# A convolution and SwiGLU kernel: one unit's x loads twelve steps later, their second copy twenty steps later, and the start's filler matmuls regrouped from six and a short one, then three, to eight, then four

## The chip, the cores and the metric

The kernel runs on one core of a Trainium2 chip. The metric is device microseconds (us) of one execution; the number given for a kernel is the median of its runs. TensorE is called PE in the profile, VectorE DVE, ScalarE ACT, GpSimd POOL and SyncE SP. POOL and SP both issue transfers; SP's transfers are issued in the order of its program, and so are POOL's, between POOL's arithmetic.

## The reference

A causal convolution with seven taps, whose taps are a softmax per head, runs over the sequence; its result goes through a gated feed-forward block.

```python
w = weight - np.max(weight, axis=-1, keepdims=True)      # weight: 8 heads x 7 taps
w = np.exp(w)
w = w / (np.sum(w, axis=-1, keepdims=True) + 1e-09)
x_pad = np.concatenate([np.zeros((B, pad, D)), x], axis=1)   # x: 8 x 4096 x 192, pad 6
x_unf = x_pad[:, idx, :].reshape(B, S, K, H, group)
out = np.einsum('hk,bskhg->bshg', w, x_unf)
...
g = x @ w_gate                                            # 192 -> 1536
silu = g * (1.0 / (1.0 + np.exp(-g)))
val = x @ w_val
return (silu * val @ w_out)                               # 1536 -> 192
```

## The kernel before, in words

The 32,768 tokens are cut into 16 units of 2,048 tokens, and each unit into four blocks of 512. For each block the feed-forward part takes twelve steps, one for each 128 of the 1,536 inner features, so that there are 768 steps in all; they are counted by n, and a unit is 48 steps. Block 0 starts at n = 0, unit 1 at n = 48, block 5 at n = 60, unit 2 at n = 96.

A step (`gate_val`, line 765) is six matmuls (line 774: gate and val, three slices of 64 channels each), a Silu on ACT (line 783, kept as `silu[n]`) and a product on DVE (line 785). Every third step a `slot` (line 833) adds a group of down-projection matmuls (line 800); the fourth slot of a block evicts the result (lines 858 and 859) and SP writes it out (line 862). PE takes everything in program order.

The convolved x of each unit is made in one of three ways.

- Unit 0 is made at the start by PE (`early`, `eturn`), with taps spread into a matrix (`spread_taps`, line 287, and `make_wide`, line 315).
- Unit 2 alone is convolved by PE with a banded matrix (`conv_half`, line 450): POOL loads overlapping windows of x into the tile x16 (`load_x`, line 129, transfers of line 98: one of 26 x 192 elements after a small memset, one of 32 x 39 x 192, one of 32 x 40 x 192), SP copies each of its two 32-row parts to the next 32 rows (`dup_x`, line 144, two transfers of 480 KB, line 148), and at n = 58 and n = 70 PE multiplies (line 466), which ACT and DVE evict into tm (line 483). POOL then copies 64 columns of tm (`conv_dup`, line 494), SP writes tm to HBM (`conv_out`, lines 502 and 510) and reads it back transposed (`fetch`, line 524) as the xc that the steps from n = 96 on read.
- Unit 1 and units 3 to 15 are "pooled": POOL's queue casts x into HBM (`cast_x`, line 580), SP reads it back transposed (line 595) and joins halves (line 599), and ACT, DVE and POOL multiply and add the taps (`conv_job`, line 614; POOL's additions are line 627, its products line 642). A unit has six such jobs. For unit 1 POOL takes four taps of the six that are added in each job. SP then moves the results into place (`place`, line 687, four transfers per block, line 701). The first of them for block 4 and block 5 reach SP's program at n = 38 and n = 48.

The order on each engine is written out by hand: the helper `seq` (line 73) ties each instruction to the one recorded before it on the same engine. The step loop (line 896) decides where something stands: it calls `gate_val`, the slot, `pooled_work` (line 740) and then the loads of x16, the copies `dup_x` and the jobs of `plan`. An instruction of a late engine therefore runs later than its n suggests: POOL and SP lag behind PE. The loads carry a wait for `silu[n - 1]`, so that they don't start early.

At the start PE runs filler matmuls on a zero tile (`keep_warm`, line 872) while the taps are computed: six of 512 columns and one of 128 ahead of `spread_taps`, three of 256 columns behind it, ahead of `make_wide`.

Of the kernel before, what the change touches and what calls it, by code (L numbers as in the profile page):

```python
# [10 lines left out]
def kernel(  # L11
# [23 lines left out]
    P = 128  # L35
# [37 lines left out]
    def seq(i):  # L73

        e = i.ins.engine
        if e in last_on:
            tc.add_manual_dep(i.ins, last_on[e].name, NOSYNC, reason="order")
        last_on[e] = i.ins
        return i
# [64 lines left out]
    def dup_x(u, queue=None):  # L144
        for r in range(2):
            p0 = Q * r
            seq(
                (queue or nc.sync).dma_start(
                    out=x16[u][p0 + 32 : p0 + 64], in_=x16[u][p0 : p0 + 32]
                )  # L150
            )
# [135 lines left out]
    def spread_taps():  # L287
        bank = apool.tile([P, TB], fp32, tag="acc0", name="tapbank")
        for a in range(2):
            seq(  # L290
                nc.tensor.matmul(
                    bank[:, a * H : a * H + H],
                    split[:, a].rearrange("h k q -> h (k q)"),
                    eye[0:H, 0:H],
                    start=(a == 0),
                    stop=True,
                    skip_group_check=True,
                )
            )
        seq(nc.vector.tensor_copy(tap, bank[:, 0 : 2 * H]))  # L300
        seq(
            nc.vector.tensor_tensor(
                spread.rearrange("p j a h -> p j (a h)"),
                eyes,
                tap.unsqueeze(1).to_broadcast([P, 16, 2 * H]),
                op=ALU.mult,
            )
        )
# [6 lines left out]
    def make_wide():  # L315
        banks = [
            ppool.tile([P, TB], fp32, tag=tag, name="taps") for tag in ("gate", "val")
        ]
        for n in range(4):
            c0 = 16 * 2 * H * (n % 2)  # L320
            seq(
                nc.tensor.matmul(
                    banks[n // 2][:, c0 : c0 + 16 * 2 * H],
                    shift[:, n].rearrange("p r i -> p (r i)"),
                    spread.rearrange("p j a h -> p (j a h)"),
                    start=(n % 2 == 0),
                    stop=True,
                    skip_group_check=True,
                )
            )  # L330
        seq(nc.vector.tensor_copy(pf, pid))
        for h0 in (0, 4):
            for n in range(2):
                seq(
                    (nc.scalar.copy, nc.vector.tensor_copy)[n](
                        wide[:, :, h0 : h0 + 4, 32 * n : 32 * n + 32],
                        banks[n].rearrange("p (j a h) -> p a h j", a=2, h=H)[
                            :, :, h0 : h0 + 4, :
                        ],
                    )  # L340
                )
        seq(
            nc.vector.tensor_scalar(
                ident, cid, scalar1=pf, scalar2=None, op0=ALU.is_equal
            )
        )
# [80 lines left out]
    def eturn(b, where):  # L427
        xc[b] = []
        for k in range(SL):
            t = cpool.tile([P, XW], fp16, tag=f"xc{k}", name=f"xc{k}", bufs=6)  # L430
            pool, tag = where[k]
            bank = pool.tile([P, EG, P], fp16, tag=tag, name="turn")
            for g in range(EG):
                seq(
                    nc.tensor.transpose(  # L435
                        bank[:, g, :], tme[b][:, g, Q * k : Q * k + P], ident
                    )
                )
            seq(
                (dve, act, dve)[k](  # L440
                    t.rearrange("p (g c j) -> p g c j", c=2, j=EO),
                    bank.rearrange("p g (c q) -> p g c q", c=2)[:, :, :, 0:EO],
                )
            )
            xc[b].append(t)
# [94 lines left out]
    def make_picks():  # L540
        for name in which:
            pick[name] = small(f"pick_{name}", [H, P], fp16)
            seq(
                nc.vector.scalar_tensor_tensor(
                    pick[name], which[name], float(grp), above[name],
                    op0=ALU.is_lt, op1=ALU.mult,
                )
            )
# [154 lines left out]
    def pooled(u):  # L703
        return u in POOLED
# [60 lines left out]
    def gate_val(n):  # L765
        b, j = divmod(n, NCH)
        g = ppool.tile([P, TB], fp32, tag="gate", name="gate")
        v = ppool.tile([P, TB], fp32, tag="val", name="val")
        m, e = divmod(j, E)
        for k in range(SL):  # L770
            for half, o in ((0, g), (1, v)):
                p0 = Q * half
                seq(
                    nc.tensor.matmul(  # L774
                        o,
                        w16[m][p0 : p0 + Q, (k + half) % SL, e::E],
                        xc[b][k][p0 : p0 + Q, 0:TB],
                        start=(k == 0),
                        stop=(k == SL - 1),
                    )  # L780
                )
        sg = hpool.tile([P, TB], fp16, tag="sig", name="sig", bufs=3)
        silu[n] = seq(nc.scalar.activation(sg, g, AF.Silu)).ins  # L783
        hj = hpool.tile([P, TB], fp16, tag="h", name="h", bufs=15)
        seq(nc.vector.tensor_tensor(hj, sg, v, op=ALU.mult))  # L785
        hbuf[n] = hj
# [85 lines left out]
    def keep_warm(count, width=TB):  # L872
        for _ in range(count):
            seq(
                nc.tensor.matmul(  # L875
                    warm[:, 0:width], fill,
                    fill.unsqueeze(1).to_broadcast([P, width // P, P]),
                    start=True, stop=True, skip_group_check=True,
                )
            )  # L880

    gate_bank, val_bank = (ppool, "gate"), (ppool, "val")
    acc_banks = (apool, "acc0"), (apool, "acc1")
    keep_warm(6)
    keep_warm(1, P)
    spread_taps()
    keep_warm(3, 2 * P)
    make_wide()
    early(0, (gate_bank, gate_bank, val_bank))
    eturn(0, (*acc_banks, gate_bank))  # L890
# [5 lines left out]
    for n in range(n_steps):  # L896
        b, j = divmod(n, NCH)
        u, ls = divmod(n, ustep)
        work = None
        if n in (12, 19):  # L900

            def work(e=2 if n == 12 else 3):
                early(e, (gate_bank, gate_bank, val_bank))

        at = (10, 22)
        if u + 1 < NU and not pooled(u + 1) and ls in at:

            def work(u=u, hh=at.index(ls)):
                conv_half(u + 1, hh)

        gate_val(n)
        if n == 6:
            early(1, (*acc_banks, gate_bank))
        elif n == 8:
            eturn(1, (*acc_banks, gate_bank))
        elif n in (9, 12, 15, 17):
            k = {9: 1, 12: 2, 15: 3, 17: 4}[n]
            slot(k, 0, silu[n - 1 if k == 4 else n - 2], work)
        elif j % 3 == 1 and n > 18:
            if j == 4 and act_steps and act_steps[0][0] < (  # L920
                dve_steps[0][0] if dve_steps else n_jobs[0]
            ) + 3:
                act_steps.pop(0)[1]()
            k = {1: 3, 4: 4, 7: 1, 10: 2}[j]
            slot(k, b - 1 if j < 7 else b, silu[n - 2], work)
        if n == 18:
            eturn(2, (*acc_banks, gate_bank))
        elif n == 20:
            eout(3)
        elif n == 21:  # L930
            efetch(3)
        if n == 10:
            make_picks()
        if n == 13:
            make_channel_taps()
        pooled_work(n, j, work is not None)
        if u + 1 < NU and not pooled(u + 1):
            if ls == at[0]:
                conv_dup(u + 1)
            if ls == at[1]:  # L940
                for m in range(2):
                    conv_out(u + 1, m)
            if ls == at[1] + 1:
                for m in range(2, 8):
                    conv_out(u + 1, m)
            if ls in range(28, 40, 3):
                fetch(UB * (u + 1) + (ls - 28) // 3)
        if u + 2 < NU and not pooled(u + 2):
            if ls == (16 if u == 0 else 1):
                x16_tile(u + 2)  # L950
                load_x(u + 2, 0, silu[n - 1])
            if ls == (18 if u == 0 else 5):
                load_x(u + 2, 1, silu[n - 1])
            if ls == (31 if u == 0 else 26):
                dup_x(u + 2)
        for job in plan.pop(n, ()):
            job()
    b = n_blocks - 1
# [41 lines left out]
```

## Time and profile before

| what | value |
|---|---|
| median of 5 runs | 780.39 us (779.04 to 782.48) |
| the profiled execution's own time | 780.39 us |
| its span | 778.6 us |
| granted TensorE clock over the span | 0.999 |
| PE / DVE / ACT / POOL busy | 99% / 88% / 78% / 84% |
| POOL busy in 36 to 56, 56 to 76, 76 to 96 us | 19.32, 19.33, 19.33 of 20.00 us |
| PE busy in 112 to 120 us | 5.62 of 8.00 us |
| the chain that ended last | PE 93%, POOL 3%, SP's queue 1%, DMA 1% |

The span begins at the program's first instruction and ends with its last one; the remaining 1.8 us of the execution's time lie around it. A busy share of PE counts matmuls that are pipelined, so that 99% does not mean that nothing can be gained in a stage; waits and the order of time show where a stage is held up. Rows of a timeline give the start, the length, the engine ("SPq" for SP's queue of instructions, where the length is that of the issue and not of the transfer), the line, the operation, the tiles and how many instructions were merged; a bracket gives the idle time before the row and what ended it.

### The profile page before, as it was taken

Reading aid. Unit: us, or ns where it says so; the run is one execution under the profiler, and the core shown is the slowest. Engines: PE = TensorE matmul, PEld = TensorE weight load, DVE = VectorE, ACT = ScalarE, POOL = GpSimd, SP = SyncE. Lnnn points to the kernel's source line nnn. Section 1 sums busy time; section 2 is a strip of 40 time slices with the busy share of each in tenths; the row PEclk is TensorE's granted clock in tenths of the full one; section 3 lists DMA queues with packets and bytes.
Section 4 is the critical chain, followed back from the end, with each engine's and each line's share of the span. In section 5 each row is a group of like instructions: output and inputs, shape, how many; then the busy total and the mean of one; then the engine's idle time right before and its main releaser. Section 6 shows DMA issues by size and latency. Waiting matters only on the chain.

```text
span 778.6 us, 27795 instructions
## 1 busy us (share of the span) xinstructions
PE 767.4 (99%) x11113; PEld 590.5 (76%) x11113; DVE 687.5 (88%) x1036; ACT 609.9 (78%) x1075; POOL 651.1 (84%) x600
## 2 busy tenths in 40 slices
PE   8999989999999999999999999999999999999997
PEld 5667657777777777777777777777777777777776
DVE  7687879999999999999999999999999999997775
ACT  6676868888888788788788788788888888886664
POOL 8299987989999999899999999999999989994000
PEclk9999999999999999999999999999999999999999
DMA  9975384752544546354442653634353452221211
GB/s 159 143 126 134 80 145 104 155 116 76 122 101 99 107 87 117 78 122 93 104 112 58 136 104 84 122 85 105 91 118 91 108 111 60 70 68 37 70 56 43
DMA packets 135678, 77.78 MB, mean 100 GB/s; under 512 B 82036, under 2 KB 135036, under 8 KB 135036
## 3 DMA queue, kind: packets, MB, share of 16 engines
q1 hardware_dynamic: 127884, 61.22, 34.9%
q0 software_dynamic: 7664, 14.79, 11.6%
q8 instruction: 87, 1.43, 0.8%
q14 instruction: 43, 0.35, 0.1%
HBM read 29.58 MB, written 37.58 MB: 86 GB/s over the span
## 4 chain that ended last, share of the span: by engine, by line
PE 93%; POOL 3%; SPq 1%; DMA 1%; issue 0%; ACT 0%; DVE 0%; POOLq 0%
PE gate L774 50%; PE acc L800 31%; PE val L774 11%; POOL total L627 2%; SPq L524 1%; POOL piece L642 1%; PE warm L875 0%; DMA xc<-scr 0%; PE turn L435 0%; PE cv L377 0%; SPq L701 0%; PE acc L821 0%; DMA pxc<-pxc 0%; POOL y L627 0%; DVE h L785 0%
## 5 line engine op out<-in xcount | busy, mean ns | idle before, releaser
L785 DVE TENSOR_TENSOR h<-sig,val 128x512 f16<-128x512 f16 x768 | 496.7, 684 | 82.8 <-PE val L774 49.8
L783 ACT ACTIVATE sig<-gate 128x512 f16<-128x512 f32 x768 | 446.9, 600 | 152.3 <-PE val L774 125.4
L774 PE MATMUL gate<-pxc,w 64*128 64x512 f16 x2016 | 471.8, 376 | 0.8 <-DMA pxc<-pxc 0.8
L774 PE MATMUL val<-pxc,w 64*128 64x512 f16 x2016 | 471.6, 376 | 0.3 <-DMA pxc<-pxc 0.3
L774 PEld LDWEIGHTS <-w 64*128 64x128 f16 x4608 | 319.9, 110 | 131.3 <-issue 4.3
L800 PEld LDWEIGHTS <-h 64*128 64x128 f16 x6096 | 273.7, 94 | 44.6 <-ACT sig L783 11.8
L800 PE MATMUL acc<-wo,h 64*128 64x192 f16 x6096 | 303.3, 243 | 1.5 <-ACT sig L783 1.2
L627 POOL TENSOR_TENSOR total<-total,part 128x512 f32<-128x512 f32 x136 | 173.1, 1273 | 31.9 <-DVE total L652 23.5
L627 POOL TENSOR_TENSOR total<-total,piece 128x512 f32<-128x512 f32 x122 | 170.8, 1400 | 10.2
L642 POOL TENSOR_SCALAR piece<-x,both_taps 128x512 f32<-128x512 f16 x206 | 168.9, 820 | 0.0
L652 DVE SCALAR_TENSOR_TENSOR total<-x,both_taps,total 128x512 f32<-128x512 f16 x162 | 168.4, 1040 | 0.0
L677 ACT ACTIVATE part<-x,both_taps 128x512 f32<-128x512 f16 x136 | 97.6, 718 | 0.0
L627 POOL TENSOR_TENSOR pxc<-total,piece 128x512 f16<-128x512 f32 x56 | 72.3, 1292 | 4.7
L774 PE MATMUL gate<-xc,w 64*128 64x512 f16 x288 | 68.9, 377 | 2.4 <-DMA xc<-scr 2.4
L774 PE MATMUL val<-xc,w 64*128 64x512 f16 x288 | 68.7, 377 | 0.1
L677 ACT ACTIVATE total<-x,both_taps 128x512 f32<-128x512 f16 x84 | 60.5, 720 | 4.6 <-DMA x<-xs 3.3
L627 POOL TENSOR_TENSOR y<-total,piece 128x512 f16<-128x512 f32 x28 | 46.6, 1663 | 2.3
L859 DVE COPY o_sb<-acc 128x384 f32<-128x384 f32 x63 | 34.7, 551 | 0.0
L858 ACT COPY o_sb<-acc 128x384 f32<-128x384 f32 x63 | 29.6, 470 | 0.1
L98 POOL DMA_DIRECT2D x<-in_x_dram x3 | 2.3, 777 | 9.2 <-ACT sig L783 9.2
L580 POOL DMA_DIRECT2D xs<-in_x_dram x14 | 7.8, 557 | 0.0
L98 POOL DMA_DIRECT2D xe<-in_x_dram x9 | 6.1, 685 | 0.1
(68 smaller groups left out, 61.3 us busy)
## 6 DMA issues: line engine op xcount, KB each, us to landing
out_dram<-o_sb SPq DMA_DIRECT2D x63, 384.0 KB
pxc<-pxc SPq DMA_DIRECT2D x112, 64.0 KB
pxc<-y SPq DMA_DIRECT2D x112, 64.0 KB
xs<-in_x_dram POOLq DMA_DIRECT2D x8, 774.0 KB, 7.1
xs<-in_x_dram POOLq DMA_DIRECT2D x6, 768.0 KB, 6.9
x<-x SPq DMA_DIRECT2D x28, 66.0 KB
x<-xs SPq DMA_TRANSPOSE x112
x<-x SPq DMA_DIRECT2D x2, 480.0 KB
```

The source lines that it names most:

```text
L98: nc.gpsimd.dma_start(out=t[p0 + i0 : p0 + i1, w0 - at : w1 - at, :], in_=bass.AP(tensor=x_flat.tensor, offset=(t0 + size * w0 - pad + i0) ...
L580: nc.gpsimd.dma_start(out=flat[skip * D : rows * D].rearrange("(a n) -> a n", n=n), in_=bass.AP(tensor=x_flat.tensor, offset=(u * UT - XP ...
L627: nc.gpsimd.tensor_tensor(job["dst"] if k == K - 1 else total, total, part, op=ALU.add)
L642: nc.gpsimd.tensor_scalar(part, shifted(k), scalar1=job["tap"][:, k : k + 1], scalar2=1.0, op0=ALU.mult, op1=ALU.mult,)
L652: nc.vector.scalar_tensor_tensor(job["total"], shifted(k), job["tap"][:, k : k + 1], job["total"], op0=ALU.mult, op1=ALU.add,)
L677: nc.scalar.activation(part, shifted(k), AF.Copy, scale=job["tap"][:, k : k + 1])
L774: nc.tensor.matmul(o, w16[m][p0 : p0 + Q, (k + half) % SL, e::E], xc[b][k][p0 : p0 + Q, 0:TB], start=(k == 0), stop=(k == SL - 1),)
L783: silu[n] = seq(nc.scalar.activation(sg, g, AF.Silu)).ins
L785: seq(nc.vector.tensor_tensor(hj, sg, v, op=ALU.mult))
L800: nc.tensor.matmul(acc[b][bank][:, s, :], hj[p0 : p0 + Q, ts(2 * bank + s, P)], wo16[p0 : p0 + Q, j, :], start=(not second and j == 0 and ...
L858: seq(nc.scalar.copy(o_sb[:, 0:2, :], acc[b][0]))
L859: seq(nc.vector.tensor_copy(o_sb[:, 2:4, :], acc[b][1]))
```

## The change

The two loads of unit 2's x move from n = 16 and n = 18 to n = 28 and n = 30; the second copy of it moves from n = 31 to n = 51, seven steps ahead of the first matmuls that read it. At the start PE's fillers become eight of 512 columns ahead of the taps, and four of 256 columns behind them. No arithmetic of the result is changed.

```diff
-    keep_warm(6)
-    keep_warm(1, P)
+    keep_warm(8)
     spread_taps()
-    keep_warm(3, 2 * P)
+    keep_warm(4, 2 * P)
     make_wide()
...
         if u + 2 < NU and not pooled(u + 2):
-            if ls == (16 if u == 0 else 1):
+            if ls == (28 if u == 0 else 1):
                 x16_tile(u + 2)
                 load_x(u + 2, 0, silu[n - 1])
-            if ls == (18 if u == 0 else 5):
+            if ls == (30 if u == 0 else 5):
                 load_x(u + 2, 1, silu[n - 1])
-            if ls == (31 if u == 0 else 26):
+            if u and ls == 26:
                 dup_x(u + 2)
+        if n == 51 and not pooled(2):
+            dup_x(2)
         for job in plan.pop(n, ()):
             job()
```

In the order of the built program, POOL's memset and three loads stood behind the cast of unit 1 and ahead of the first addition of unit 1's first job; they now stand behind the last addition of its second job (the one that writes y for blocks 4 and 5) and ahead of the first addition of its third (block 5). SP's two copies stood ahead of the four transfers that place block 4; they now stand behind those of blocks 4 and 5 and behind one transposing read of unit 3.

## The prediction

> **What bounds the kernel now.** I read the page first, then the chain of work that ended last, then the timelines of POOL, SP's queue and PE over the first 120 us, where everything that the change touches lies. The page says that PE is the bound over the whole span, so the end moves only if some wait of PE moves.
>
> ```profile
> PE 767.4 (99%) x11113; PEld 590.5 (76%) x11113; DVE 687.5 (88%) x1036; ACT 609.9 (78%) x1075; POOL 651.1 (84%) x600
> ```
>
> The chain between 75 and 120 us (start, length, what) shows the last such wait.
>
> ```profile
> 104.80 5.92 SPq L524
> 110.76 2.80 SPq L524
> 113.60 2.69 DMA xc<-scr
> 116.33 0.37 PE gate L774
> ```
>
> After 116.33 the chain is PE alone up to the end. PE waits there, at n = 96, for unit 2's xc, read by the transposes of line 524. Whatever changes the time of that matmul changes the end by as much; earlier waits count only if they reach it. Without a wait its gate matmul would have come at about 113.4 (the gates before it, at 112.33, 112.55 and 112.76, lie 0.215 apart, and it is the third one on), so PE has 2.9 us of slack there.
>
> What sets the data's time is POOL. Its timeline (start, length, line, tiles, idle time before):
>
> ```profile
> 17.46 0.25 POOL L133 MEMSET x<- 6x192 f16 x1
> 26.08 1.45 POOL L98 DMA_DIRECT2D x<-in_x_dram  x2 [8.37 <-ACT sig L783]
> 28.36 0.87 POOL L98 DMA_DIRECT2D x<-in_x_dram  x1 [0.83 <-ACT sig L783]
> 35.63 1.27 POOL L627 TENSOR_TENSOR total<-total,part 128x512 f32<-128x512 f32 x1 [6.40 <-DVE total L652]
> ...
> 54.63 1.58 POOL L627 TENSOR_TENSOR y<-total,piece 128x512 f16<-128x512 f32 x1
> 56.18 1.27 POOL L627 TENSOR_TENSOR total<-total,part 128x512 f32<-128x512 f32 x1
> ...
> 64.72 1.27 POOL L627 TENSOR_TENSOR pxc<-total,piece 128x512 f16<-128x512 f32 x1
> ```
>
> The loads of x16 lie before 29.3, in time in which POOL has nothing else: after them it still waits 6.40 us for DVE. From 35.63 it has no idle bracket until 113.17; the windows give 19.3 busy of 20 us. Every instruction put into that stretch delays all that follows. Behind it hang the last results of unit 1 (95.25), the copy of tm (95.18 to 96.44) and the cast for unit 4 (103.89). SP follows at once: its transfers of block 7 begin at 95.27, those of line 502 at 97.75, the read that PE waits for at 104.80. That read took 5.92 us to issue, and the second 2.80, where undisturbed ones take 1.25: the cast, issued at 103.89, landed at 111.44. The earlier cast (45.40, landed 52.76) held two reads of line 595 in the same way (2.66 and 4.41). Both SP's writes and this cast come from POOL's queue.
>
> SP's timeline around the second copy:
>
> ```profile
> 54.40 1.27 SPq L595 DMA_TRANSPOSE x<-xs  x1
> 55.84 2.31 SPq L148 DMA_DIRECT2D x<-x  x2
> 58.24 1.84 SPq L701 DMA_DIRECT2D pxc<-pxc  x1
> 60.13 2.84 SPq L701 DMA_DIRECT2D pxc<-y  x2
> ...
> 66.02 0.47 SPq L701 DMA_DIRECT2D pxc<-pxc  x1
> ```
>
> The copies stand ahead of block 4's transfers, which PE needs at 62.6, and their landing records are at 61.34 and 63.71. Block 5's first transfer, at 66.02, goes when POOL has ended its result (64.72 + 1.27 = 65.99).
>
> **The change, part by part.**
>
> *Fillers.* Six fillers of 512 columns start 0.427 us apart from 0.98, the short one starts at 3.51, and the tap matmul at 3.76 waits for DVE. Eight hold PE to about 4.37, 0.6 later. The four behind end near 5.36 (0.213 each), so the matmuls of line 322 start at 5.36 instead of 4.56; the full clock is first recorded at 5.40, so I let three of them run at half of their 0.213 and count 0.4 for what follows. The first step's second matmul waited for a weight transfer, until 8.74 instead of about 8.56, and gives back some 0.2. Left: **+0.2** (0 if the full clock comes sooner, +0.6 if nothing is given back). PE is busy on from there to POOL's first addition, so this shift reaches POOL.
>
> *Loads moved on POOL.* The wait for `silu[15]` goes, and DVE is late next: POOL still starts at 35.63. Nothing is gained. The memset and the three loads now stand between 56.18 and what followed it: 0.25 + 1.45 + 0.87 = 2.57, with gaps **+2.6**. Bounds: four times nothing is excluded, since the cast at 45.40 held POOL for its full 0.58; three times the shortest load of line 98 (0.53) and the memset give 1.8, three times the longest (0.93) give 3.05. Their waits (`silu[27]`, `silu[29]`) are long over by 56. POOL's chain is thus 2.8 late.
>
> *Loads and copies out of SP's way.* Block 4's transfers can go at 56.4, when y is done, and land before PE's need: of the six matmuls of n = 48 (62.62 to 65.11, 2.49 instead of 0.65) 1.84 us return. The reading that ACT waited for at 50.92 (3.27) was behind a chain of SP transfers that landed late beside the x loads, and may come ahead of the cast. DVE's evictions at 43.23, 56.80 and 70.16 lie 13.57 and 13.36 apart, where undisturbed blocks take 11.73 (95.18 to 106.91): up to 3.5 us return before n = 58. All of it is lost again in the next part.
>
> *The second copy.* It stands behind block 5's transfers, which now wait for POOL until 65.99 + 2.8 = 68.8. Their four issues take 2.4 (as at 95.27 to 97.66) and the read of line 595 1.3, so the first copy issues at 72.5. Before, the second had landed 7.9 after the first's issue, also behind one such read; so now at 80.4. PE reached this multiplication at 75.35 and now comes to it at 75.35 + 0.2 - 3.5 = 72.1. It is the next instruction in PE's order, with all steps from n = 59 on behind it, and ACT and DVE wait for PE. PE stands still for some 8.3 us and goes on 80.4 - 75.35 = **5.1** late. Bounds: the copies' packets themselves ran from 58.0 to 62.7, so 4.7 and an issue of 0.5 would give 77.7 (+2.3); with the slower issues of block 5 in this trace (66.02 to 69.07) 81.1 (+5.8).
>
> *The clock after that stop.* No stop of this length is in the trace. PE's longest break with the clock staying full is the one at n = 96 (2.9 in two waits): price 0. After the idle time at the start, the fillers ran at half speed from 0.98 to the record at 5.40, 4.42 us, which at half speed loses 2.2. The stop is almost three times the longest one survived, so I take the start's row: **+2.2**, and keep 0 as the other end.
>
> The Trainium skill (TensorE: Matmul & The Clock Gate, Part 1) says that the clock halves after an idle window of about 3.4 us and comes back after a busy one. No run here shows the first half of that; the start's 4.42 us agrees with the second. By the rule the loss would be an estimated 1.7 to 3.4 us, since a window runs freely, and without the rule it could be nothing.
>
> *The sum at n = 96.* PE's side: 5.1 + 2.2 - 2.9 of slack = +4.4. The data's side: POOL's 2.8, or more if DVE is late for it: unit 3's first job needs a DVE product that ended at 93.32, and 93.32 + 7.3 = 100.6 is 1.4 later than POOL's 96.40 + 2.8, so +4.2. The later one counts: +4.4. The profiled execution took 780.39, which is also the median of the five runs; **784.8 us**.
>
> **The rivals.**
>
> *The clock stays full* (or the copies are 2 us quicker). Then PE's side is 5.1 - 2.9 = +2.2, POOL's +2.8 decides: 783.2. For it: the trace shows no lowered clock after the first 5.4 us. Against: the length of the stop.
>
> *It hardly shows.* The loads cost 1.8, the fillers nothing, and the cast lands in 7.04 (as the one of 16.88 did) instead of 7.55: +1.3, 781.7. It needs the clock full and the copies landed by 79.5 as well.
>
> *Faster.* The reads of line 524 slip out of the cast's hold. Two issues of 1.25 for 5.92 and 2.80 are worth 6.2 us, so the data would be there at 116.3 + 2.8 - 6.2 = 112.9, and PE's own arrival decides; it gains only if the copies land before 76 or so, and with no wait for them the end comes 3.4 earlier: 777.0. Against: cast and reads both hang on POOL and keep their distance of 0.9.
>
> *Slower still.* The copies share the transfer engines with more than before and land past 82, or the cold stretch is 7 us: each us past 80.4 counts in full. Two more give 787.
>
> That the loads don't come "twelve steps" later is sure: twelve steps are some 12 us, and on POOL it is 30, because POOL lags.
>
> **How the numbers follow.** Forecast 0.50, clock full 0.22, hardly shows 0.13, slower still 0.08, faster 0.07. The range leaves out most of "faster" and half of "hardly shows" below, and the end of "slower still" above: 781.8 to 786.9. A change of 0.3% (2.34 us) is about what a measurement of this kernel tells from none: forecast, slower still and nearly all of "clock full" lie above 782.7, together 0.79; faster than 778.0 is 0.07; within is 0.14.
>
> **What would show it.** Right: POOL's three loads between 56 and 60 with no idle time; block 5's result near 68.8; no wait of PE at n = 48; a wait of several us ahead of line 466 until about 80, with matmuls of half speed behind it; the matmul of 116.33 near 120.7. Wrong: POOL's first addition well before 35.6, or the first read of line 524 short, or line 466 without a wait.

## The result, and the profile after

The changed kernel takes 783.55 us (median of 53 runs, 782.54 to 784.86), the kernel before, run beside it on the same chips, 780.93 us (95 runs, 779.04 to 786.17). The ratio is 1.0028, with a 95% interval of 1.0021 to 1.0035. (The ratios and intervals given here are taken over the runs and are not the quotient of the two medians, which is 1.0034 here; the two can differ by up to 0.2%.) So the change makes the kernel slower, by 2.6 us of median; whether that is over 0.3% can't be told, since the interval lies across that bound. The forecast was 784.8, the range 781.8 to 786.9.

The profiled execution of the changed kernel took 784.86 us (span 783.1) and was the slowest of its runs. That of the kernel before (780.39) was half a us under its median. Between these two executions the difference is 4.47 us, and the sum of the prediction, which was made for the profiled execution, said 4.4. Both numbers count below: the profiles show the mechanism, and the medians show what it is worth.

From the page of the changed kernel (section 1, section 4's shares of the chain that ended last by engine, and the row of the banded matmuls in section 5: busy time, mean ns, idle time before and what ended it):

```profile
PE 769.1 (98%) x11115; PEld 520.4 (66%) x11115; DVE 685.9 (88%) x1036; ACT 610.1 (78%) x1075; POOL 649.0 (83%) x600
...
PE 97%; DMA 1%; ACT 1%; SPq 1%; DVE 0%; issue 0%; POOL 0%; POOLq 0%; ACTq 0%
...
L466 PE MATMUL cv<-x,band 64*32 64x240 f16 x64 | 2.2, 331 | 7.0 <-DMA x<-x 7.0
```

POOL had 3% of the chain before and rounds to none now, and 7.0 us of idle time stand ahead of line 466, where there were none. POOL's timeline of the changed kernel (start, length, line, tiles, idle time before):

```profile
36.65 1.26 POOL L627 TENSOR_TENSOR total<-total,part 128x512 f32<-128x512 f32 x1 [18.61 <-DVE total L652]
...
55.59 1.27 POOL L627 TENSOR_TENSOR y<-total,piece 128x512 f16<-128x512 f32 x1
56.79 0.25 POOL L133 MEMSET x<- 6x192 f16 x1
57.00 2.38 POOL L98 DMA_DIRECT2D x<-in_x_dram  x3
59.39 1.76 POOL L627 TENSOR_TENSOR total<-total,part 128x512 f32<-128x512 f32 x1
...
68.46 1.27 POOL L627 TENSOR_TENSOR pxc<-total,piece 128x512 f16<-128x512 f32 x1
```

The memset and the three loads stand in a row without idle time and take 2.60 us (56.79 to 59.39). Block 5's result ends at 69.73; before it ended at 65.99. SP's queue of the changed kernel takes up from there (start, length of the issue):

```profile
69.75 0.47 SPq L701 DMA_DIRECT2D pxc<-pxc  x1
70.27 1.23 SPq L701 DMA_DIRECT2D pxc<-y  x2
71.54 0.59 SPq L701 DMA_DIRECT2D pxc<-pxc  x1
72.23 1.21 SPq L595 DMA_TRANSPOSE x<-xs  x1
73.56 1.22 SPq L148 DMA_DIRECT2D x<-x  x2
```

The two copies are issued at 73.56 and 74.23; by the trace's records of transfers that ended, they landed at 77.88 and 80.13. PE's timeline of the changed kernel shows who waited for them:

```profile
71.78 1.15 PE L800 MATMUL acc<-wo,h 64*128 64x192 f16 x24
78.01 0.35 PE L466 MATMUL cv<-x,band 64*32 64x240 f16 x1 [5.08 <-DMA x<-x]
80.26 1.00 PE L466 MATMUL cv<-x,band 64*32 64x240 f16 x31 [1.90 <-DMA x<-x]
```

PE stands still for 5.08 us, runs one matmul when the first copy is there, and stands still for 1.90 more. The windows of the changed kernel tell what follows (start:end, length, then busy time and count of PE, PEld, DVE, ACT and POOL, granted clock, DMA share, GB/s):

```profile
75.00:80.00 5.00, 0.35 (x1) 0.10 (x1) 0.00 (x0) 0.00 (x0) 4.83 (x5) 0.50 0.85 181
80.00:85.20 5.20, 4.94 (x59) 2.55 (x61) 1.91 (x3) 1.89 (x4) 4.95 (x7) 0.50 0.39 101
85.20:90.00 4.80, 4.80 (x70) 3.17 (x68) 3.30 (x6) 3.38 (x7) 4.72 (x5) 1.00 0.45 98
```

The granted clock is half from 74.99 to 85.23. PE has work again from 80.26 on, so that five us of it run at half speed: the gate matmuls are 0.427 apart there and 0.215 later. At n = 96 PE does not wait. The matmul that stood at 116.33 stands at 120.81 without a bracket, and the last read that it needs landed at 119.18 (PE's timeline of the changed kernel):

```profile
120.81 0.38 PE L774 MATMUL gate<-xc,w 64*128 64x512 f16 x1
```

One number makes the rest short. From that matmul (the third gate matmul of n = 96) to the span's end it takes 662.2 to 662.4 us in each of the 14 profiles of this study. Whatever a version does, it shows in the time of this matmul and nowhere behind it; "n = 96" below means that time.

### The profile page after: what moved, and what is told of

Its sections match the earlier page's. It is cut to its first block, busy times and chain, and to the rows that moved or that the text cites. A ratio compares the mean times of both kernels' runs of the same rounds, so it can differ in the third digit from the quotient of the medians.

```text
span 783.1 us, 27799 instructions
## 1 busy us (share of the span) xinstructions
PE 769.1 (98%) x11115; PEld 520.4 (66%) x11115; DVE 685.9 (88%) x1036; ACT 610.1 (78%) x1075; POOL 649.0 (83%) x600
## 4 chain that ended last, share of the span: by engine, by line
PE 97%; DMA 1%; ACT 1%; SPq 1%; DVE 0%; issue 0%; POOL 0%; POOLq 0%; ACTq 0%
PE gate L774 61%; PE acc L800 32%; PE val L774 2%; DMA x<-x 1%; PE warm L875 1%; PE turn L435 0%; PE cv L377 0%; ACT sig L783 0%; PE acc L821 0%; SPq L701 0%; DVE h L785 0%; PE cv L466 0%; DVE o_sb L859 0%; POOL pxc L627 0%; SPq L595 0%
## 5 line engine op out<-in xcount | busy, mean ns | idle before, releaser
L774 PEld LDWEIGHTS <-w 64*128 64x128 f16 x4608 | 254.9, 110 | 183.8 <-issue 2.3
L800 PEld LDWEIGHTS <-h 64*128 64x128 f16 x6096 | 259.0, 94 | 58.5 <-ACT sig L783 12.7
L800 PE MATMUL acc<-wo,h 64*128 64x192 f16 x6096 | 294.6, 243 | 0.9 <-ACT sig L783 0.8
L652 DVE SCALAR_TENSOR_TENSOR total<-x,both_taps,total 128x512 f32<-128x512 f16 x162 | 166.6, 1028 | 0.0
L483 DVE CAST tm<-cv 128x480 f16<-128x480 f32 x4 | 2.4, 648 | 7.7 <-PE cv L466 7.7
L483 ACT CAST tm<-cv 128x480 f16<-128x480 f32 x4 | 2.0, 562 | 9.1 <-PE cv L466 9.1
L466 PE MATMUL cv<-x,band 64*32 64x240 f16 x64 | 2.2, 331 | 7.0 <-DMA x<-x 7.0
```

The costliest lines, as they stand in the source:

```text
L483: eng(tm[u][:, NG * r : NG * r + NG, 2 * grp * hp : 2 * grp * hp + 2 * grp].rearrange("p g (t e) -> p g t e", t=2), banks[r][:, 0 : 2 * w] ...
L652: nc.vector.scalar_tensor_tensor(job["total"], shifted(k), job["tap"][:, k : k + 1], job["total"], op0=ALU.mult, op1=ALU.add,)
L774: nc.tensor.matmul(o, w16[m][p0 : p0 + Q, (k + half) % SL, e::E], xc[b][k][p0 : p0 + Q, 0:TB], start=(k == 0), stop=(k == SL - 1),)
L800: nc.tensor.matmul(acc[b][bank][:, s, :], hj[p0 : p0 + Q, ts(2 * bank + s, P)], wo16[p0 : p0 + Q, j, :], start=(not second and j == 0 and ...
```

## The experiments

Each version was run beside the kernel before on the same chip. Diffs are against the kernel before unless the text says otherwise.

### The two halves of the change

The fillers alone, with loads and copies where they were:

```diff
-    keep_warm(6)
-    keep_warm(1, P)
+    keep_warm(8)
     spread_taps()
-    keep_warm(3, 2 * P)
+    keep_warm(4, 2 * P)
```

> The kernel before, with only the fillers changed (eight of 512 columns ahead of the taps, four of 256 behind). Theory: the fillers hold the start back, and POOL's first addition and all behind it move by that, since PE is busy from there to it. The prediction put this at +0.2 us; the profiled execution of the changed kernel shows the first Silu at 10.52 instead of 9.51 and the full clock at 6.73 instead of 5.40, which would be +1.0. So 0.2 to 1.0 us over before, and POOL's first addition between 35.8 and 36.7. Rival: the fillers' cost is swallowed by PE's wait at n = 96 (2.9 us of slack), and the time is that of before within 0.1 us.

Measured: 780.28 us beside 780.74, ratio 0.9991 (0.9975 to 1.0007). The fillers cost nothing that can be measured. In its profile the first Silu comes at 9.68 (before 9.51, after 10.52), so that most of the us by which the profiled execution after is late at the start belongs to that execution and not to the fillers. A part may be theirs: in the five profiles with the new fillers the first Silu comes at 9.68 to 10.52, in the nine with the old ones at 9.44 to 9.88 (five) or 10.58 to 11.45 (four).

Loads and copies moved as in the change, fillers as before:

```diff
-            if ls == (16 if u == 0 else 1):
+            if ls == (28 if u == 0 else 1):
...
-            if ls == (18 if u == 0 else 5):
+            if ls == (30 if u == 0 else 5):
...
-            if ls == (31 if u == 0 else 26):
+            if u and ls == 26:
                 dup_x(u + 2)
+        if n == 51 and not pooled(2):
+            dup_x(2)
```

> The changed kernel with the fillers of before: only the loads and the second copy are moved. Theory: the copy's stop of PE ahead of line 466 (7 to 8 us) and the half-speed clock behind it make nearly all of the loss, so 1.6 to 2.6 us over before, with a stretch of lowered clock of about 10 us and no wait at n = 96. Rival: the fillers are the larger part, and this kernel is less than 1 us over before.

Measured: 783.52 beside 780.74, ratio 1.0033 (1.0017 to 1.0048). The moves carry the whole cost. n = 96 is at 120.07.

### The copies without the loads

The second copy at n = 51, the loads where they were:

```diff
-            if ls == (31 if u == 0 else 26):
+            if u and ls == 26:
                 dup_x(u + 2)
+        if n == 51 and not pooled(2):
+            dup_x(2)
```

> The kernel before with only the second copy moved to n = 51; loads and fillers stay. POOL keeps its times, so block 5's result is there at 66.0, the copies issue near 70 and land near 77.7, 2.6 us sooner than in the changed kernel. Theory: PE stops for 4 to 6 us and goes on 2.3 us later than before; if the clock halves again, PE's side is 2.3 + 2.2 - 2.9 = +1.6 (782.5), if it doesn't, PE's wait at n = 96 swallows it (780.9). Rival: the loads on POOL don't matter for the copy's place, and this kernel is as slow as the one with both moved.

Measured: 781.51 beside 780.74, ratio 0.9998 (0.9982 to 1.0015). Without POOL's loads in the way, block 5's result ends at 66.39, the second copy lands at 77.16, and PE hardly waits for it (PE's timeline of this version):

```profile
77.30 0.60 PE L466 MATMUL cv<-x,band 64*32 64x240 f16 x31 [0.22 <-DMA x<-x]
```

So the same place in SP's program costs nothing that can be measured as long as POOL is on time, and the loss takes both moves. The short wait is in part luck of this execution: PE came late to line 466 (at 76.80, behind a wait for ACT of 2.3 us and a clock at half from 60.29 to 63.71). At the 75.35 of before it would have waited for some 2 us, less than the slack that the prediction saw at n = 96.

### The loads late, but the copies between blocks 4 and 5

After, with one number changed:

```diff
-        if n == 51 and not pooled(2):
+        if n == 40 and not pooled(2):
             dup_x(2)
```

> The changed kernel, with the second copy at n = 40: behind block 4's transfers and ahead of block 5's in SP's queue. The copies then wait for the loads, which land near 69, and land near 75, about 5 us sooner than at 80. Theory: PE's stop shrinks to 2 or 3 us, the clock stays full, PE's side falls below the data's side, and POOL's delay (2.6 us of loads and the fillers' 0.2 to 1.0) is what is left: 2.8 to 3.6 us late at n = 96 in the profile, with a wait of PE there again, and a time no better than 1 us below the changed kernel (782.5 to 784.5). Rival: POOL's loads are hidden and the stop alone costs: then the time falls to that of the fillers alone, 781.1 to 781.9.

Measured: 782.40 beside 780.74, ratio 1.0025 (1.0005 to 1.0045). The copies land at 73.32, and line 466 starts at 73.99, ahead of the 75.35 of before. But n = 96 now waits for its data, which is late with POOL (PE's timeline of this version; idle time and releaser in the bracket):

```profile
117.43 0.40 PE L774 MATMUL gate<-xc,w 64*128 64x512 f16 x1 [1.18 <-DMA xc<-scr]
...
118.09 0.37 PE L774 MATMUL gate<-xc,w 64*128 64x512 f16 x1 [0.26 <-DMA xc<-scr]
```

The last read landed at 118.60, 2.31 later than the 116.29 of before; n = 96 is at 118.65. This is what the rival "the clock stays full" named as the next bound: POOL's delay alone costs 1.7 us of median (782.40 and 780.74; by the interval of the ratio 0.4 to 3.5), even where the copies are in time. The clock did fall once in this profile, from 91.25 to 94.67, behind a wait of 1.57 us for block data (`pxc<-y`, until 90.20), but the wait at n = 96 swallows that.

### What the cold clock costs

After, with fillers on the zero tile ahead of the first banded matmul, so that PE has work during the stop. They write into a PSUM bank that line 466 then starts anew.

```diff
+            if hp == 0:
+                for _ in range(24):
+                    seq(
+                        nc.tensor.matmul(
+                            banks[0], fill,
...
```

> The changed kernel, with 24 matmuls of 512 columns on the zero tile put ahead of the first multiplication of line 466 (they write a bank that this multiplication then starts anew). They take 24 x 0.215 = 5.2 us of the time in which PE stands still for the second copy. Theory: the clock stays full, the steps behind the stop run at full speed (2.5 us less), and the end gains until the data's side decides: in the changed kernel's profile the last read landed at 119.2 and was used at 120.8, so 1.6 us faster than the changed kernel, 781.5 to 782.5. Rival: the lowered clock cost nothing that counts, and the time stays at 783.5.

Measured: 783.97 beside 781.16, ratio 1.0024 (1.0009 to 1.0038): no change against after. The clock fell all the same, so this version doesn't tell what the cold clock costs. PE's timeline of it shows why (its line 475 is line 466 of the others, and line 464 the fillers):

```profile
72.19 5.35 PE L464 MATMUL cv<-fill 128*128 128x512 f16 x24
77.89 0.26 PE L475 MATMUL cv<-x,band 64*32 64x240 f16 x1 [0.35 <-DMA x<-x]
80.20 0.60 PE L475 MATMUL cv<-x,band 64*32 64x240 f16 x31 [2.05 <-DMA x<-x]
```

The fillers end with the first copy; the 2.05 us behind it stayed, and the clock was half from 81.17 to 84.58. With 36 fillers instead of 24 the stop is filled to its end (against the version above):

```diff
-                for _ in range(24):
+                for _ in range(36):
```

> The changed kernel with 36 matmuls on the zero tile in PE's stop instead of the 24 of the earlier run, where 2.3 us of idle time stayed behind them and the clock halved at 81.2 for 3.4 us. They take 7.7 us and end near 79.9, where the second copy lands at 80.1. Theory: no idle time over 1 us is left, the clock stays full, the 2.1 to 2.5 us of half speed behind the stop go, and the end gains 1.5 to 2.5 us over the changed kernel (781.0 to 782.0). Rival: the half-speed stretch isn't what counts at n = 96, and the time stays at 783.5.

Measured: 782.75 beside 781.81, ratio 1.0011 (0.9995 to 1.0028). PE's timeline of this version, and its windows for the same stretches as above (clock in the third column from the right):

```profile
72.24 7.94 PE L464 MATMUL cv<-fill 128*128 128x512 f16 x36
80.11 0.84 PE L475 MATMUL cv<-x,band 64*32 64x240 f16 x32
```

```profile
75.00:80.00 5.00, 5.00 (x25) 2.15 (x22) 0.00 (x0) 0.00 (x0) 4.83 (x6) 1.00 0.84 178
80.00:85.20 5.20, 5.20 (x97) 3.41 (x98) 3.20 (x5) 2.84 (x6) 4.95 (x6) 1.00 0.53 132
```

The clock stays full, and from the banded matmul's start to n = 96 it takes 38.19 us (80.11 to 118.30) instead of 40.55 (80.26 to 120.81). In these two profiles the cold clock is worth 2.4 us. By the medians it is 0.8 us (783.55 to 782.75), or 1.3 by the two ratios, and their intervals overlap. The end can gain less than the clock gives back, since the data's side is close: the last read landed 1.63 us ahead of its matmul in the changed kernel (119.18 and 120.81) and 0.94 in this version (117.36 and 118.30). That this is what makes the difference was not tested.

The granted clocks on record, for 54 executions of the changed kernel, say how often the clock falls. Over the span they are 0.992 to 0.996 in all but one (0.998), with the 36 fillers 0.999 or 1.000 in all twelve. The 15 executions with 0.992 or 0.993, the profiled one among them, took 784.3 us on average, the 38 with 0.994 to 0.996 took 783.2.

### Whether the kernel before has its slack in every execution

The prediction gave PE 2.9 us of slack at n = 96. The copy moved to n = 40 alone, with loads as before, was to free block 4's transfers:

```diff
-            if ls == (31 if u == 0 else 26):
+            if ls == (40 if u == 0 else 26):
```

> The kernel before with only the second copy moved, to n = 40: behind block 4's transfers and ahead of block 5's. The loads landed long before, so the copies issue near 59 and land near 66, ahead of PE's need at 73. Theory: the wait at n = 48 (1.8 us) goes, no stop comes ahead of line 466, and all of it is given back at n = 96, where the data still come at 116.3 by POOL and the cast: the time of before within 0.5 us, with a longer wait at n = 96 (near 4.7 us). Rival: what PE gains at n = 48 stays gained: 1.8 us faster.

Measured: 780.89 beside 781.16, ratio 0.9995 (0.9978 to 1.0012). The wait at n = 48 went, but a wait of ACT at 56 had grown (ACT's timeline of this version, bracket as above):

```profile
56.23 0.72 ACT L677 ACTIVATE total<-x,both_taps 128x512 f32<-128x512 f16 x1 [4.51 <-DMA x<-xs]
```

PE stood still behind it, the clock was half from 57.86 to 61.27, and n = 96 was at 118.78. The same wait is 3.27 in the profile of before; in the other versions that leave the loads and the cast for unit 3 in place it lies between 0.16 and 6.59, and where it is 0.16 (the fillers alone) a wait of 4.50 on the join of line 599 follows at 59.14. What ACT waits for is a read of line 595 or the join behind it; that the cast for unit 3 holds them is tested below. So there may be a hold for each of two casts, and one for the copies. The next five versions take them away one by one.

The cast for unit 4 nine steps later (from n = 77 to n = 86), so that the reads of line 524 go ahead of it:

```diff
-            plan.setdefault(s0 - (120 if v == 3 else 115), []).append(
+            plan.setdefault(s0 - {3: 120, 4: 106}.get(v, 115), []).append(
```

> The kernel before with only the cast for unit 4 nine steps later (n = 86). Theory: the reads land near 110, PE comes to n = 96 at 113.4 without a wait and the wait of 2.9 us goes: 778.0. Rival: the cast doesn't hold the reads, 780.9.

Measured: 780.57 beside 781.16, ratio 0.9980 (0.9964 to 0.9997). SP's timeline of this version has all six reads in one go, and in PE's the first matmul of n = 96 has no bracket, so that it does not wait:

```profile
104.49 7.78 SPq L524 DMA_TRANSPOSE xc<-scr  x6
```

```profile
116.47 0.38 PE L774 MATMUL gate<-xc,w 64*128 64x512 f16 x1
```

The reads' issues take 1.27, 1.26 and 1.26 where before one took 5.92, and the last of the three that n = 96 needs landed at 109.82 instead of 116.29. Yet n = 96 is at 116.90, because ACT waited 2.07 at 50.19 and 4.28 at 59.47 and the clock was half from 62.17 to 65.58. The data is 6.5 us earlier, and it is worth a fifth of a per cent by the ratio and 0.6 us by the medians.

The same with the copies at n = 40 as well:

```diff
+            plan.setdefault(s0 - {3: 120, 4: 106}.get(v, 115), []).append(
...
+            if ls == (40 if u == 0 else 26):
```

> The kernel before with the second copy at n = 40 and the cast for unit 4 nine steps later (n = 86), so that on POOL it stands behind unit 3's second job. Theory: the reads of line 524 that unit 2 starts with are no longer held by the cast, land near 110 instead of 116.3, and PE comes to n = 96 without a wait at 113.4 - 1.8 = 111.6: 4.7 us faster than before, near 776.3. Rival: the cast doesn't hold the reads (SP's own writes and the output do), and the time stays at 780.9.

Measured: 781.05 beside 781.16, ratio 0.9981 (0.9962 to 1.0000). In its profile ACT's wait for the reads of unit 3 is 6.59, PE's behind it 4.8, and n = 96 is at 118.57 with its data there at 111.33. This profile is of one of the longer executions (782.64): four of the twelve took 777.3 to 778.3, near the 776.3 of the expectation, the others 779.9 to 782.7.

The cast for unit 3 four steps later (n = 28 instead of 24; on POOL it then stands behind the addition that writes y), the others as before:

```diff
-            plan.setdefault(s0 - (120 if v == 3 else 115), []).append(
+            plan.setdefault(s0 - (116 if v == 3 else 115), []).append(
```

> The kernel before with only the cast for unit 3 four steps later (n = 28), which on POOL is behind unit 1's second job (near 56 instead of 45.4). In the runs that keep the loads early, ACT waits 2 to 6.6 us between 47 and 60 for reads of line 595 that this cast holds, PE with it, and the clock halves for 3.4 to 6.8 us; where the loads come late, SP's queue is ahead of the cast and this wait is small. Theory: with the cast out of the way the wait goes, PE comes to n = 48 near 62 in this kernel too, and what is left is the data's side at n = 96: 0.5 to 1.5 us faster than before, with a wait at n = 96. Rival: the loads themselves hold these reads, and the wait stays: the time of before.

Measured: 781.08 beside 781.81, ratio 0.9999 (0.9986 to 1.0012). ACT's early waits are down to 1.37 and 0.99, which fits the cast as the holder and not the loads, and the time is spent at n = 48 instead, behind the copies (PE's timeline of this version):

```profile
63.20 0.37 PE L774 MATMUL gate<-pxc,w 64*128 64x512 f16 x1 [1.67 <-DMA pxc<-pxc]
...
65.09 0.58 PE L774 MATMUL val<-pxc,w 64*128 64x512 f16 x1 [1.51 <-DMA pxc<-y]
```

Behind these waits the clock was half from 63.58 to 70.41, and at n = 96, at 116.09, PE doesn't wait.

Both casts later, the copies as before:

```diff
-            plan.setdefault(s0 - (120 if v == 3 else 115), []).append(
+            plan.setdefault(s0 - {3: 116, 4: 106}.get(v, 115), []).append(
```

> The kernel before with both casts later: unit 3's at n = 28 and unit 4's at n = 86. Theory: neither side holds n = 96 any more, PE's early wait is gone and the reads of line 524 land near 110: the matmul of 116.3 comes at 111.5 to 113.5, 3 to 5 us faster than before (776 to 778). Rival: block 6's data, which hang on POOL (near 88), hold PE at n = 72, and half of it is lost: 778.5 to 779.5.

Measured: 781.55 beside 781.81, ratio 1.0003 (0.9989 to 1.0018). The wait at n = 48 is there as in the version above: the waits of PE list 1.5 us for `pxc<-pxc` and 1.2 for `pxc<-y`.

Both casts later, and the copies at n = 40:

```diff
+            plan.setdefault(s0 - {3: 116, 4: 106}.get(v, 115), []).append(
...
-            if ls == (31 if u == 0 else 26):
+            if ls == (40 if u == 0 else 26):
```

> As the last one, and the second copy at n = 40, behind block 4's transfers. Theory: the copies, issued near 59, land near 66, ahead of PE's need at 72, and block 4's transfers go as soon as POOL has ended y: PE comes to n = 96 at 111 to 112, 4 to 5 us faster than before (776 to 777). Rival: POOL's block 6 decides, and there is no difference from the kernel with both casts later alone.

Measured: 778.31 (776.05 to 781.05) beside 781.81, ratio 0.9957 (0.9940 to 0.9974). This version beats both kernels. Its profile is of its slowest execution, in which the start was slow (first Silu at 11.45), and even so the list of PE's waits between 36 and 120 us holds no transfer at all (the 2.0 us end at 40.89, the profile shows no cause for them, and the clock is half from 40.87 to 44.28):

```profile
PE acc L800 <- issue: 2.0, 1, 2.0
PE val L774 <- DVE h L785: 0.7, 1, 0.7
```

The list of before for the same stretch has 2.4 us at n = 96 and 1.1 at n = 48 (0.8 and 0.3), and 1.2 for ACT.

| version | ratio to before (95%) | what is left in its profile |
|---|---|---|
| after | 1.0028 (1.0021 to 1.0035) | stop at line 466, cold clock |
| fillers only | 0.9991 (0.9975 to 1.0007) | ACT's waits, cold clock after them |
| moves only | 1.0033 (1.0017 to 1.0048) | stop at line 466, cold clock |
| after, 24 fillers in the stop | 1.0024 (1.0009 to 1.0038) | the rest of the stop, cold clock |
| after, 36 fillers in the stop | 1.0011 (0.9995 to 1.0028) | stop, clock full |
| after, copies at n = 40 | 1.0025 (1.0005 to 1.0045) | late data at n = 96 |
| copies at 51, loads early | 0.9998 (0.9982 to 1.0015) | ACT's waits, cold clock after them |
| copies at 40, loads early | 0.9995 (0.9978 to 1.0012) | the same |
| cast 4 later | 0.9980 (0.9964 to 0.9997) | the same |
| cast 4 later, copies at 40 | 0.9981 (0.9962 to 1.0000) | the same |
| cast 3 later | 0.9999 (0.9986 to 1.0012) | n = 48, cold clock after it |
| both casts later | 1.0003 (0.9989 to 1.0018) | n = 48 |
| both casts later, copies at 40 | 0.9957 (0.9940 to 0.9974) | none of the three |

The loads late with the copies left ahead of block 4 were not tried, nor the cast for unit 3 together with the copies, nor the best version with the new fillers.

## Why the prediction was right, and where it was not

- **n = 96 decides the end: right**, to 0.2 us over all profiles. That PE's side would decide there and not the data was right for the change: PE is there at 120.81 without a wait, the data at 119.18.
- **Loads, +2.6: right.** They take 2.60, without idle time, and block 5's result ends 3.74 later: 1.02 from the start, 2.6 from the loads, 0.1 between.
- **The wait at n = 48 goes, and PE comes early to line 466: right.** PE ended its work at 72.93 (78.01 - 5.08); the prediction had 72.1, and the start's 1.0 explains the rest.
- **The second copy, +5.1: right.** It landed at 80.13 (forecast 80.4), and the multiplication goes on 4.91 later than before (80.26 and 75.35). That it is so close is in part luck: the first copy was issued at 73.56 (forecast 72.5), and the second landed 6.57 after that and not 7.9. The stop is in two pieces, 5.08 and 1.90, since the first matmul needs the first copy alone.
- **The clock, +2.2: right in its nature, and about right in this execution** (2.4 against the version with 36 fillers; 4.97 us of work at half speed lose 2.5). In most executions it is worth less at the end: the medians give 0.8 to 1.3, and the executions with the higher granted clock are 1.0 us faster. The break of before that the prediction took for 2.9 us has 2.36 us of idle time (1.44 and 0.92).
- **Fillers, +0.2: the size failed in the profile and held in the mean.** Between the two profiled executions the start moved by 1.0, and the full clock came at 6.73 and not near the 5.40 of before, but the fillers alone show no cost (ratio 0.9991, up to 1.0007 by its interval).
- **The data's side, +2.8 or +4.2: the lower one held.** The last read landed 2.89 later (119.18 and 116.29), and 2.31 later in the version where PE was early.

Of the rivals, "it hardly shows" fails on the loads (2.60 and not 1.8), "faster" on the reads of line 524, which the cast holds again (5.76), and "slower still" on the copies, which landed at 80.13 and not past 82. "The clock stays full" (783.2) is what the version with 36 fillers (782.75) and the one with the copies at n = 40 (782.40) come near.

The sum met the profiled execution (784.86) and lies 1.25 us over the median. By the constant of 662.3 and the 1.8 around the span, a median of 780.93 means n = 96 at about 116.8, and 783.55 means 119.4. So the change costs 2.6, and not 4.4, between the medians: the profile after was an unlucky one by 1.3, and the one before a lucky one by 0.5. That the two profiles lie apart by what the sum gives is luck to that extent. For the 1.3 the granted clocks point to the clock's term: the profile after has 0.992, which goes with the longer executions. How much of it is the later start was not separated.

For the 0.5 it is the start of the sum, PE's slack of 2.9 us at n = 96. It was read from one execution, and in that one it was there. In the profiles of four versions that leave the loads where they were (the fillers alone, the copies at n = 40, and the cast for unit 4 later, without and with the copies at n = 40), PE comes to n = 96 at 116.8 to 118.8 without a wait, in the last two although the data is there 7 us earlier. ACT waits 4.3 to 6.6 us in these for reads or for the join behind them, PE waits behind ACT, and the clock falls for 3.4 to 6.8 us. The cast held two reads in the trace of before as well, and the prediction quoted them (2.66 and 4.41), but took ACT's wait there as something that may vanish and not as a second bound. In these versions PE also comes to line 466 later, at 78.8 to 80.5 and not at 75.35 (in two of them a late start, with the first Silu at 10.72 and 11.11, adds to it), so that a copy landing at 80.1 costs less there; this would be why a missing slack of 2.9 moves the sum by so little.

That other executions of the kernel before go the same way is argued, since it has one profile. What is on record fits: of its 105 executions beside the experiments, 55 had a granted clock of 0.997 or less and took 782.1 us on average, the 19 with 0.999 or 1.000 took 780.0. The profiled one had 0.999.

That the change removes such an early wait is also in its profile: from 36 to 70 us PE is busy for 33.16 of 34 us, where it was 31.32 before. The gain is real, and it is spent at line 466: PE arrives early there and waits.

The versions with later casts show that three holds stand in a row: the cast for unit 3 (ACT's wait at 50 to 60), the copies ahead of block 4 (n = 48), and the cast for unit 4 (n = 96). Taking away one, or two in the two pairs that were tried, moves the ratio by 0.2% at most, since the next takes up the time; all three give 0.43%. In its profile the change has neither of the first two (ACT waits 1.00 us at 55.46, where it was 3.27 at 50.92) and, by delaying POOL, has made a fourth.

## What to carry to other kernels

Before a transfer is moved on a queue, list what its issuing engine does at the new place: 2.6 us of issues cost nothing where POOL was waiting and reached PE through two queues where it was full. A slack read in one profiled execution should be checked against others, or against the spread of the runs, before it is subtracted in a sum. If taking away the wait that ends last gives nothing, look for the next hold in the row and take away all of them in one version before the idea is given up.

## What the runs showed of the hardware

- **A cast in flight from POOL's queue holds SP's transposing reads.** In the changed kernel the cast for unit 4 is issued at 107.48 and lands at 115.51, and the reads of line 524 stand in it (SP's timeline, three issues in 8.92 us):

```profile
107.74 8.92 SPq L524 DMA_TRANSPOSE xc<-scr  x3
```

The one of 109.59 took 5.76 to issue. With the cast behind them six issues took 7.78 (the cast for unit 4 later, above). Which part of the transfer path does it was not shown.
- **The clock goes by windows of 3.41 us, and one that is idle for somewhat more than half of it lets it fall.** In each of the 14 profiles the changes of the clock lie whole multiples of 3.41 us apart (in the changed kernel at 6.73, 74.99 and 85.23: 20 and 3 of them). Laid on this grid, the window ahead of the fall in the changed kernel, and the one of before that holds most of the wait at n = 96 (PE's busy time is the number behind the comma, the granted clock the third from the right):

```profile
71.58:74.99 3.41, 1.35 (x28) 1.00 (x24) 1.71 (x3) 0.94 (x2) 3.24 (x5) 1.00 0.74 162
```

```profile
111.21:114.63 3.42, 1.98 (x40) 1.40 (x35) 2.50 (x4) 1.64 (x3) 1.76 (x3) 1.00 1.15 127
```

The first was followed by half clock, the second was not. Of the windows at full clock in all profiles, the 24 in which PE was busy for 1.55 us or less were all followed by half clock, and none with 2.0 us or more was; between 1.58 and 1.98 both occur. A half-speed window was followed by full clock only where PE was busy for at least 2.92 us. So a stop's price hangs on where it falls in the grid: half-speed stretches of 3.4 us (24 fillers; copies at 40 alone), 6.8 (moves alone; cast 3 later) and 10.24 (after). The Trainium skill (TensorE: Matmul & The Clock Gate, Part 1) puts the fall after an idle window of about 3.4 us that runs freely. The length and the free run agree with this case; that the window must be idle does not, with 1.35 us of work in it here and 1.22 with the 24 fillers.
- **The start is not the same in each execution.** With the fillers of before the clock became lastingly full at 4.1 to 5.7 us in five of nine profiles, and at 9.96, 10.76, 13.48 and 13.56 in the others; in that of the best version the first steps' matmuls are 0.41 to 0.43 apart up to 13.3 us. With the new fillers that was never later than 6.73 in five profiles. The runs of after also spread less (782.5 to 784.9, before 779.0 to 786.2). That the fillers narrow the spread is argued from this and not shown.
